# A new order for the DMA queue and the engine plan of a gated two-branch spectral mixer

## The chip, the cores and the metric

The kernel runs on one core of a Trainium2 chip. The metric is the device time of one execution in microseconds, as the median of several executions. A profile is one further execution; its span runs from the first to the last instruction and is about 2 us shorter than the device time. Runs that took over 1.5% longer than the fastest of the same kernel count as slow and are left out of all ratios. The engines are called TensorE (PE in the profile; its weight loads are PEld), VectorE (DVE), ScalarE (ACT), GpSimd (POOL) and SyncE (SP), which issues nearly all DMA. The hardware page set that readers have at hand is named "the Trainium skill", with the page's title.

## The reference, cut to what matters

```python
def _A_ref(x, w_r, w_i):                      # the same for B, with its own weights
    X = jnp.fft.rfft2(x.astype(jnp.float32), axes=(-2, -1))     # x: 1 x 2048 x 1024
    X = X * (w_r + 1j * w_i)
    return jnp.fft.irfft2(X, s=(2048, 1024), axes=(-2, -1)).astype(jnp.bfloat16)

g = sigmoid((x * gate_w).sum(-1, keepdims=True))
return g * A_ref(x) + (1 - g) * B_ref(x)
```

Both branches transform the same x, so the forward transform is done once and the two inverse ones are mixed by the gate before the last step.

## The kernel before

Every transform is a set of matmuls with constant matrices. The kernel has five steps, each in sixteen pieces:

- **f1**: first forward transform, straight from x. Its result needs sums and differences of column halves, done on VectorE ("fold"), on GpSimd ("pool") or by further matmuls ("sum").
- **f2, f3**: the rest of the forward transform, for the even half of the columns (units 0 to 7) and the odd half (units 8 to 15).
- **c1, c2, ce**: products with the spectral weights W on VectorE, and small corrections on GpSimd.
- **i1**: first inverse step. Its result is copied to SBUF and stored to a DRAM scratch (`hb`), from which it is read back in another layout (`rb`): half 0 into `re`, half 1 into `ro`.
- **i2, then ev, of, od, ol**: the gate and second inverse step on what was read back, then the last step and the stores (`st`).

The program is written out by hand. A plan lists the pieces, and each engine executes its instructions in the plan's order:

```python
PLAN = """
lw 3; lw 4; lw 5; f1 0; f1 3; ...            # lw: load weights W of a unit
... i1 7 1; f2 10 0; c1 8 w; hb 6; lw 15; ...
... i1> 13 1 A; i2 0 1; hb 12; c2 14 w; f3 15 w; f3> 15 w A; i2 0 0     # first readback units
"""
```

The pieces that the argument touches (cuts marked):

```python
def load_w(n):
    par, u = n // NU, n % NU
    k = n % 11                                # eleven slots: a later unit takes an earlier unit's slot
    ...
    nc.sync.dma_start(w, w_in[par][u].rearrange("p t a m -> p (t a) m"))

def i1_out(n):                                # hb: store of unit n to the scratch
    nc.sync.dma_start(HB[par][16 * u:16 * u + 16]. ... , PS.pop(("rl", n))[:])

def read_back(par, s0, n=2):                  # rb: slots s0 and s0 + 1 of half par
    nc.sync.dma_start(RR[par][:, s0:s0 + n, :], HB[par][:, s0:s0 + n, :])

def i2(par, v, eng="A"):                      # unit v reads slots 2v and 2v + 1
    for s in range(2):
        ps = one()[:]
        s1 = 2 * v + s
        for ch in range(4):
            for ab, Ew in enumerate((EA, EB)):
                nc.tensor.matmul(ps[:, ch * 128:ch * 128 + 128],
                                 lhsT=RR[par][:, s1, ...], rhs=Ew[:, s1, :], ...)     # line 543
        copy(eng[s % len(eng)], ...)

def pair(o, a, b, engs="DD"):                 # line 554: D = VectorE, P = GpSimd
    for k, op in enumerate((ALU.add, ALU.subtract)):
        (nc.vector if engs[k] == "D" else nc.gpsimd).tensor_tensor(o[:, :, k], a, b, op)
```

Of the kernel before, what the change touches and what calls it, by code (L numbers as in the profile page):

```python
# [12 lines left out]
D = 1024  # L13
# [122 lines left out]


F1_GROUPS = """
0 fold 0 0 2 0
1 pool 0 1 1 1  # L140
3 pool 1 1 1 s
2 fold 2 0 2 1
4 pool 2 1 1 s
6 fold 4 0 2 1
5 pool 3 1 1 s
7 fold 6 0 2 0
# [2 lines left out]
13 pool 5 1 1 s  # L149
10 fold 10 0 2 1  # L150
11 fold 12 0 2 0
14 sum 14 0 1 s
15 sum 15 0 1 s
16 pool 6 1 1 s
17 pool 7 1 1 s
18 fold 8 1 2 1
19 sum 10 1 2 1
20 sum 12 1 1 s
21 fold 13 1 1 0
22 fold 14 1 1 s  # L160
# [12 lines left out]
ce 2; f3 3 w; i1> 1 0 A; i1> 1 2 D; f2> 4 1 A; fs> 3; f3> 3 w A; i1> 1 1 A; f1+ 20; f1 23; c2 2 w; c1 3 w; f2 4 0
f1> 23 A; i1 2 0; ce 3; f2> 4 0 A; lw 6; hb 0; lw 8; f1+ 23; i1 2 1; c2 3 w; i1> 2 0 A; i1> 2 1 A; f3 4 w; lw 7; fs 4
lw 10; f3> 4 w A; f2 5 0; fs> 4; f2> 5 0 A; f2 5 1; i1> 2 2 D; f2> 5 1 A; c1 4 w; i1 3 0; hb 1; i1 3 1; i1> 3 0 A
ce 4; fs 5; f3 5 w; i1> 3 1 A; f3> 5 w A; hb 2; i1> 3 2 D; f2 6 0; fs> 5; f2> 6 0 A; f2 6 1; hb 3; i1 4 0; c2 4 w
lw 11; i1 4 1; f2> 6 1 D; f3 6 w; lw 12; i1> 4 0 A; c1 5 w; fs 6; f2 7 0; ce 5; i1> 4 2 D; fs> 6; f2 7 1; c2 5 w
i1 5 0; i1> 4 1 A; f3> 6 w A; lw 14; c1 6 w; hb 4; ce 6; ie; f2> 7 0 A; i1 5 1; f2> 7 1 A; fs 7; gh; i1> 5 0 A
i1> 5 2 D; fs> 7; i1> 5 1 A; f3 7 w; gh> A; f2 8 0; f3> 7 w A; f2 8 1; i1 6 0; hb 5; c2 6 w; i1 6 1; f2> 8 0 A
f2> 8 1 A; c1 7 w; i1> 6 0 A; i1> 6 1 A; lw 13; i1> 6 2 D; f3 8 w; f2 9 0; c2 7 w; f2 9 1; ce 7; f3> 8 w A; f2> 9 0 A  # L180
f2> 9 1 D; i1 7 0; i1 7 1; f2 10 0; c1 8 w; hb 6; lw 15; i1> 7 0 A; i1> 7 1 A; f3 9 w; i1 8 0; i1> 7 2 D; f3> 9 w A
f2 10 1; c2 8 w; i1 8 1; f2> 10 0 A; f2> 10 1 A; f2 11 1; f3 10 w; c1 9 w; i1> 8 0 A; i1> 8 2 D; f2 11 0; hb 7; rb 0 8
c2 9 w; i1> 8 1 A; i1 9 0; rb 0 0; i1 9 1; hb 8; f3> 10 w A; f2> 11 0 D; rb 0 4; f2> 11 1 A; i1> 9 0 A; rb 0 12
i1> 9 1 A; c1 10 w; i1> 9 2 D; f2 12 1; rb 0 10; hb 9; f2> 12 1 A; f3 11 w; f3> 11 w A; f2 12 0; f2> 12 0 A; i1 10 0
c2 10 w; rb 0 6; i1 10 1; f2 13 0; c1 11 w; i1> 10 0 A; i1> 10 2 D; f2 13 1; i1> 10 1 A; f3 12 w; i1 11 0; rb 0 2
f2> 13 0 A; f3> 12 w A; f2 14 0; c2 11 w; f2> 13 1 D; i1 11 1; gz 0 0; f2 14 1; i1> 11 0 A; hb 10; f3 13 w; c1 12 w
gz> 0; i1> 11 1 A; i1> 11 2 D; c2 12 w; f2> 14 1 D; gw 0; i1 12 0; f2> 14 0 D; rb 0 14; hb 11; f3> 13 w A; c1 13 w
c2 13 w; i1 12 1; i1> 12 0 A; i1> 12 1 A; f2 15 1; i1> 12 2 A; gw 1; f2 15 0; f2> 15 1 A; f3 14 w; f3> 14 w A
f2> 15 0 A; i1 13 0; i1 13 1; i1> 13 0 A; c1 14 w; i1> 13 1 A; i2 0 1; hb 12; c2 14 w; f3 15 w; f3> 15 w A; i2 0 0
i1> 13 2 D; i1 14 0; i1 14 1; i1> 14 0 A; gz 1 0; i1> 14 1 A; hb 13; c1 15 w; i1> 14 2 D; i2 0 2; i1 15 0; c2 15 w  # L190
i1 15 1; i1> 15 0 A; gz> 1; i1> 15 1 D; i1> 15 2 D; gw 2; phase; hb 14; i2 0 3; hb 15; ev 0 1; rb 1 0; rb 1 2; ev 1 0
i2 0 4; gw 3; ev 3 1; rb 1 8; i2 0 5; rb 1 4; ev 2 0; ev 4 1; i2 0 7; i2 0 6; i2 1 0; of 0 0; rb 1 12; i2 1 1; ev 5 1
rb 1 6; i2 1 2; of 1 1; i2 1 3; rb 1 10; st 0; rb 1 14; ev 6 0; of 2 1; ev 7 1; i2 1 4; od 3 0; i2 1 5; st 3; st 2
od 4 1; od 5 1; st 1; i2 1 6; st 4; st 5; i2 1 7; ol 6; ol 7
"""


# [484 lines left out]
```

## Time and profile before

| | before |
|---|---|
| device time, median of 3 runs | 126.56 us (125.37 to 126.69) |
| span of the profile | 123.9 us |
| first inverse product (i1) starts on TensorE | 26.05 us |
| first i2 unit of half 0 starts | 75.67 us |
| first i2 unit of half 1 starts | 94.84 us |
| busy: TensorE, VectorE, ScalarE, GpSimd | 86, 77, 71, 34% |

The chain, the waits and the queue of this kernel are shown and read in the prediction below.

### The profile page before, as it was taken

What the parts mean: (1) busy time and instruction counts of PE and PEld (TensorE: products, weight loads), DVE (VectorE), ACT (ScalarE), POOL (GpSimd) and SP (SyncE); (2) the same over time, 40 slices, a digit from 0 to 9 for tenths busy, and PEclk for the clock granted to TensorE, in tenths of its full rate; (3) what the DMA queues carried; (4) which work ended last, traced back from release to release, by engine and by line L of the source; (5) the groups of instructions that cost most, each with busy time, mean ns of one, the idle gap of its engine ahead of it and who ended that gap; (6) DMA issues with size and microseconds to landing.
All of it is one profiled execution on the core that took longest, in us unless ns stands there. A gap on an engine that the chain in (4) does not pass through costs nothing.

```text
span 123.9 us, 3786 instructions
## 1 busy us (share of the span) xinstructions
PE 106.5 (86%) x1582; PEld 71.8 (58%) x1582; DVE 95.5 (77%) x139; ACT 88.5 (71%) x140; POOL 41.9 (34%) x58
## 2 busy tenths in 40 slices
PE   6999999998889899999896835999997999999700
PEld 2799996863545434534354405767986898656200
DVE  0089987799998995999999994275895368999820
ACT  4068466587989998999998992779968696606300
POOL 1059957361135555200000000000000099996520
PEclk9999999999999999999999995599999999999996
DMA  3999999999997899997499999905479921841994
GB/s 94 310 393 415 376 405 409 392 404 398 405 400 253 231 284 368 401 400 285 83 312 418 398 402 393 356 23 177 167 257 415 413 108 50 295 171 50 403 385 177
DMA packets 18289, 37.41 MB, mean 302 GB/s; under 512 B 1756, under 2 KB 10848, under 8 KB 18272
## 3 DMA queue, kind: packets, MB, share of 16 engines
q1 hardware_dynamic: 17808, 36.97, 80.8%
q10 hardware_dynamic: 432, 0.20, 0.6%
q8 instruction: 12, 0.20, 0.6%
q14 instruction: 5, 0.04, 0.1%
q0 software_dynamic: 32, 0.01, 0.0%
HBM read 24.58 MB, written 12.58 MB: 300 GB/s over the span
## 4 chain that ended last, share of the span: by engine, by line
PE 50%; DVE 15%; DMA 12%; ACT 11%; issue 5%; SPq 1%; DVEq 1%; ACTq 0%
PE ps L543 10%; DMA re<-h_143 9%; PE ia L514 5%; PE ps L425 3%; ACT rl L307 3%; PE ps L303 3%; ACT y L307 3%; DMA re<-in_x_dram 3%; DVE re L554 3%; DVE rl L307 2%; PE ps L334 2%; PE ib L514 2%; DVE T L307 2%; ACT X_149 L307 2%; ACT X_150 L307 2%
## 5 line engine op out<-in xcount | busy, mean ns | idle before, releaser
L554 POOL TENSOR_TENSOR ot<-re,y 128x1024 bf16<-128x1024 f32 x6 | 14.0, 2373 | 49.2 <-DVE y L554 49.2
L307 ACT CAST y<-ps 128x512 bf16<-128x512 f32 x35 | 19.3, 597 | 9.3 <-PE ps L543 7.7
L307 ACT CAST rl<-ia 128x1024 bf16<-128x1024 f32 x16 | 16.2, 1013 | 2.7 <-PE ib L514 2.3
L425 PE MATMUL ps<-fd,y 128*128 128x256 bf16 x112 | 16.3, 273 | 1.8 <-DVE T L307 0.8
L425 PEld LDWEIGHTS <-y 128*128 128x128 bf16 x128 | 11.0, 97 | 8.4 <-issue 7.0
L303 PEld LDWEIGHTS <-re 128*128 128x128 bf16 x216 | 13.1, 102 | 1.9 <-DMA re<-in_x_dram 1.2
L514 PEld LDWEIGHTS <-wi 32*64 32x64 bf16 x512 | 6.9, 104 | 9.5 <-issue 5.8
L543 PE MATMUL ps<-ea,re 128*128 128x128 bf16 x64 | 9.6, 242 | 3.2 <-DMA re<-h_143 2.8
L307 DVE CAST rl<-ib 128x512 bf16<-128x512 f32 x16 | 10.9, 686 | 1.8 <-PE ib L514 1.7
L307 ACT CAST T<-ps 128x512 bf16<-128x512 f32 x20 | 11.8, 613 | 0.6 <-PE ps L425 0.6
L543 PEld LDWEIGHTS <-re 128*128 128x128 bf16 x128 | 9.0, 110 | 4.7 <-DMA re<-h_143 3.3
L543 PE MATMUL ps<-eb,re 128*128 128x128 bf16 x64 | 9.7, 243 | 0.0
L564 PEld LDWEIGHTS <-y 128*128 128x128 bf16 x88 | 8.2, 97 | 2.0 <-issue 0.6
L307 ACT CAST rl<-ib 128x512 bf16<-128x512 f32 x16 | 9.4, 595 | 0.0
L462 PEld LDWEIGHTS <-wf 64*64 64x64 bf16 x192 | 4.9, 108 | 7.2 <-issue 5.4
L543 PEld LDWEIGHTS <-ro 128*128 128x128 bf16 x128 | 7.8, 98 | 1.3 <-issue 0.7
L543 PE MATMUL ps<-ea,ro 128*128 128x128 bf16 x64 | 8.1, 219 | 0.4 <-ACT y L307 0.4
L543 PE MATMUL ps<-eb,ro 128*128 128x128 bf16 x64 | 8.1, 219 | 0.0
L303 PE MATMUL ps<-f_89,re 128*128 128x128 bf16 x72 | 5.6, 222 | 0.4 <-DVE e_781 L451 0.4
L307 DVE CAST T<-ps 128x512 bf16<-128x512 f32 x8 | 5.5, 687 | 0.2 <-PE ps L425 0.2
L334 PEld LDWEIGHTS <-re 128*128 128x128 bf16 x80 | 4.6, 98 | 0.0
L291 DVE TENSOR_SCALAR gh<-gws 128x8 f32<-128x8 bf16 x1 | 0.2, 172 | 5.3 <-DMA gws<-in_gw_dram 5.3
(298 smaller groups left out, 262.9 us busy)
## 6 DMA issues: line engine op xcount, KB each, us to landing
h_143<-rl SPq DMA_DIRECT2D x8, 512.0 KB, 5.9
re<-h_143 SPq DMA_DIRECT2D x8, 512.0 KB, 9.2
h_144<-rl SPq DMA_DIRECT2D x8, 512.0 KB, 8.2
ro<-h_144 SPq DMA_DIRECT2D x8, 512.0 KB, 5.7
re<-in_x_dram SPq DMA_DIRECT2D x6, 512.0 KB, 7.2
out_dram<-ot SPq DMA_DIRECT2D x6, 512.0 KB, 3.6
ro<-in_we_dram SPq DMA_DIRECT2D x5, 512.0 KB, 8.2
ro<-in_wo_dram SPq DMA_DIRECT2D x5, 512.0 KB, 7.4
```

The costliest lines, as they stand in the source:

```text
L291: nc.vector.tensor_scalar(gh[:], gws[:], 0.25, None, ALU.mult)
L303: nc.tensor.matmul(o[:, q * 128:(q + 1) * 128], lhsT=x[:, s1, h * 512 + q * 128:h * 512 + (q + 1) * 128], rhs=F1[:, h * e, :], start=(h == ...
L307: (nc.scalar.copy if eng == "A" else nc.vector.tensor_copy)(out=out, in_=in_)
L334: nc.tensor.matmul(o, lhsT=x[:, s1 + s, h * 512 + (q + 2 * a) * 128:h * 512 + (q + 2 * a) * 128 + 128], rhs=F1[:, (h * e + a * r) % 2, :], ...
L425: nc.tensor.matmul(ps[:, i * 512 + q // 2 * 256:i * 512 + q // 2 * 256 + 256], lhsT=y[:, par, q, 4 * u + 2 * t:4 * u + 2 * t + 2, :, :].re ...
L462: nc.tensor.matmul(ps[hp(jh ^ tt), i * 512 + dst:i * 512 + dst + ln], lhsT=WF[hp(jh), 2 * u + tt, w, :], rhs=T[hp(jh), tt, src:src + ln], ...
L514: nc.tensor.matmul(bank[g][hp(tt)], lhsT=WI[h, 2 * u + tt, w, :], rhs=p[h, 4 * tt + row:4 * tt + row + 2, o:o + 256], start=(r == k == 0), ...
L543: nc.tensor.matmul(ps[:, ch * 128:ch * 128 + 128], lhsT=RR[par][:, s1, c0 + 256 * ab:c0 + 256 * ab + 128], rhs=Ew[:, s1, :], start=(ab == ...
L554: (nc.vector if engs[k] == "D" else nc.gpsimd).tensor_tensor(o[:, :, k], a, b, op)
L564: nc.tensor.matmul(ps[:, o:o + 256], lhsT=V[:, s, 2 * r + a, :], rhs=rhs[:, 2 * r + a, 0:256], start=(a == 0), stop=(a == 1))
```

## The change

The stated intent: each W load is issued right behind the product that frees its slot, each unit's scratch store right behind its copies, and the scratch is read back in the order of use. The diff rewrites the whole plan, and shifts some work between engines on the way. Its core, with the plan reduced to the words concerned and cuts marked:

```diff
 F1_GROUPS                       # group, kind, slot, half, count, accumulator
-23 fold 15 1 1 s
+23 sum 15 1 1 s
 ...                             # other accumulators for groups 0, 4, 14, 17
 PLAN, DMA queue only, in order
-lw 3 4 5; fd; lw 9 6; hb 0; lw 8 7 10; hb 1; hb 2; hb 3; lw 11 12 14; hb 4; ie; hb 5; lw 13; hb 6; lw 15; hb 7
-rb 0 8; rb 0 0; hb 8; rb 0 4; rb 0 12; rb 0 10; hb 9; rb 0 6; rb 0 2; hb 10; rb 0 14; hb 11; hb 12; ...
+lw 3 4 5 6; fd; lw 10 7 8; hb 0; lw 11 9; hb 1; lw 12 13 14; hb 2; hb 3; lw 15; ie; hb 4; hb 5; hb 6; hb 7
+rb 0 2; rb 0 0; rb 0 4; hb 8; hb 9; rb 0 6; rb 0 8; hb 10; rb 0 10; rb 0 14; hb 11; hb 12; rb 0 12; ...
 PLAN, GpSimd's folds of the opening, in order
-f1+ 1; f1+ 3; f1+ 5; f1+ 4; f1+ 13; f1+ 12; f1+ 16; ws; f1+ 17
+f1+ 4; f1+ 1; f1+ 3; f1+ 13; ws; f1+ 16; f1+ 5; f1+ 12; f1+ 17
 PLAN, the end
-of 0 0; ... of 1 1; ... of 2 1; ... od 3 0; ... od 4 1; od 5 1; ...
+of 0 1 PD; ... of 1 1 PP; ... of 2 1; ... od 3 0; ... od 4 1; of 5 0 DP; ...
```

The order of the i2 units of half 0 is about the same in both: 1, 0, 2, 3, 4, 5, 7, 6.

More of the change, by code (lines that the diff above doesn't have):

```diff
@@ L138 @@
 F1_GROUPS = """
-0 fold 0 0 2 0
+0 fold 0 0 2 1
 1 pool 0 1 1 1
@@ L142 @@
 2 fold 2 0 2 1
-4 pool 2 1 1 s
+4 pool 2 1 1 0
 6 fold 4 0 2 1
@@ L151 @@
 11 fold 12 0 2 0
-14 sum 14 0 1 s
+14 sum 14 0 1 1
 15 sum 15 0 1 s
 16 pool 6 1 1 s
-17 pool 7 1 1 s
+17 pool 7 1 1 0
 18 fold 8 1 2 1
@@ L160 @@
 22 fold 14 1 1 s
-23 fold 15 1 1 s
+23 sum 15 1 1 s
 """
 PLAN = """
-lw 3; lw 4; lw 5; f1 0; f1 3; f1 1; f1 4; f1> 0 A; f1+ 0; f1> 1 A; f1 2; f1> 2 D; f1> 4 A; f1 6; f1+ 1; f1> 3 A
-f1> 6 A; f1 5; f1+ 2; f1+ 3; f1> 5 A; f1 7; f1+ 5; f1+ 6; f1+ 4; f1> 7 A; f1 12; f1+ 7; f1 8; f1> 12 A; f1 13; f1> 8 A
-f1 10; f1 11; f1> 13 A; f1+ 8; f1> 10 A; f1+ 10; f1+ 13; f1> 11 D; f1 14; f1+ 12; f1 15; f1> 14 A; f1> 15 A; f1 16
-f1 18; f1+ 11; f1> 18 D; f1+ 18; f1 17; f1> 16 A; f1+ 15; f1> 17 A; f2 0 0; f2 1 w; f1+ 16; ws; f1+ 17; f2 0 1
@@ L169 @@
-f2> 0 1 D; f2> 0 0 A; f3 0 0; f3> 0 0 A; f1+ 14; f3 0 1; fs 0; f3> 0 1 D; f2> 1 w A; f1 19; c1 0 0; f1> 19 A; fs 1
-f3 1 w; fs> 1; c1 0 1; fs> 0; f2 2 w; f3> 1 w A; c2 0 w; ce 0; f1 20; c1 1 w; f2> 2 w A; f1 21; f1> 21 A; phase
-f1> 20 A; i1 0 0; ce 1; i1 0 1; fs 2; fd; f1 22; i1> 0 0 A; f1+ 19; f1+ 21; i1> 0 1 A; i1> 0 2 D; fs> 2; f3 2 w
-c2 1 w; f2 3 1; f3> 2 w A; f1> 22 A; f2> 3 1 D; f1+ 22; lw 9; c1 2 w; i1 1 0; f2 3 0; f2> 3 0 A; i1 1 1; f2 4 1; fs 3
-ce 2; f3 3 w; i1> 1 0 A; i1> 1 2 D; f2> 4 1 A; fs> 3; f3> 3 w A; i1> 1 1 A; f1+ 20; f1 23; c2 2 w; c1 3 w; f2 4 0
@@ L174 @@
-f1> 23 A; i1 2 0; ce 3; f2> 4 0 A; lw 6; hb 0; lw 8; f1+ 23; i1 2 1; c2 3 w; i1> 2 0 A; i1> 2 1 A; f3 4 w; lw 7; fs 4
-lw 10; f3> 4 w A; f2 5 0; fs> 4; f2> 5 0 A; f2 5 1; i1> 2 2 D; f2> 5 1 A; c1 4 w; i1 3 0; hb 1; i1 3 1; i1> 3 0 A
-ce 4; fs 5; f3 5 w; i1> 3 1 A; f3> 5 w A; hb 2; i1> 3 2 D; f2 6 0; fs> 5; f2> 6 0 A; f2 6 1; hb 3; i1 4 0; c2 4 w
-lw 11; i1 4 1; f2> 6 1 D; f3 6 w; lw 12; i1> 4 0 A; c1 5 w; fs 6; f2 7 0; ce 5; i1> 4 2 D; fs> 6; f2 7 1; c2 5 w
-i1 5 0; i1> 4 1 A; f3> 6 w A; lw 14; c1 6 w; hb 4; ce 6; ie; f2> 7 0 A; i1 5 1; f2> 7 1 A; fs 7; gh; i1> 5 0 A
@@ L179 @@
-i1> 5 2 D; fs> 7; i1> 5 1 A; f3 7 w; gh> A; f2 8 0; f3> 7 w A; f2 8 1; i1 6 0; hb 5; c2 6 w; i1 6 1; f2> 8 0 A
-f2> 8 1 A; c1 7 w; i1> 6 0 A; i1> 6 1 A; lw 13; i1> 6 2 D; f3 8 w; f2 9 0; c2 7 w; f2 9 1; ce 7; f3> 8 w A; f2> 9 0 A
-f2> 9 1 D; i1 7 0; i1 7 1; f2 10 0; c1 8 w; hb 6; lw 15; i1> 7 0 A; i1> 7 1 A; f3 9 w; i1 8 0; i1> 7 2 D; f3> 9 w A
-f2 10 1; c2 8 w; i1 8 1; f2> 10 0 A; f2> 10 1 A; f2 11 1; f3 10 w; c1 9 w; i1> 8 0 A; i1> 8 2 D; f2 11 0; hb 7; rb 0 8
-c2 9 w; i1> 8 1 A; i1 9 0; rb 0 0; i1 9 1; hb 8; f3> 10 w A; f2> 11 0 D; rb 0 4; f2> 11 1 A; i1> 9 0 A; rb 0 12
@@ L184 @@
-i1> 9 1 A; c1 10 w; i1> 9 2 D; f2 12 1; rb 0 10; hb 9; f2> 12 1 A; f3 11 w; f3> 11 w A; f2 12 0; f2> 12 0 A; i1 10 0
-c2 10 w; rb 0 6; i1 10 1; f2 13 0; c1 11 w; i1> 10 0 A; i1> 10 2 D; f2 13 1; i1> 10 1 A; f3 12 w; i1 11 0; rb 0 2
-f2> 13 0 A; f3> 12 w A; f2 14 0; c2 11 w; f2> 13 1 D; i1 11 1; gz 0 0; f2 14 1; i1> 11 0 A; hb 10; f3 13 w; c1 12 w
-gz> 0; i1> 11 1 A; i1> 11 2 D; c2 12 w; f2> 14 1 D; gw 0; i1 12 0; f2> 14 0 D; rb 0 14; hb 11; f3> 13 w A; c1 13 w
-c2 13 w; i1 12 1; i1> 12 0 A; i1> 12 1 A; f2 15 1; i1> 12 2 A; gw 1; f2 15 0; f2> 15 1 A; f3 14 w; f3> 14 w A
@@ L189 @@
-f2> 15 0 A; i1 13 0; i1 13 1; i1> 13 0 A; c1 14 w; i1> 13 1 A; i2 0 1; hb 12; c2 14 w; f3 15 w; f3> 15 w A; i2 0 0
-i1> 13 2 D; i1 14 0; i1 14 1; i1> 14 0 A; gz 1 0; i1> 14 1 A; hb 13; c1 15 w; i1> 14 2 D; i2 0 2; i1 15 0; c2 15 w
-i1 15 1; i1> 15 0 A; gz> 1; i1> 15 1 D; i1> 15 2 D; gw 2; phase; hb 14; i2 0 3; hb 15; ev 0 1; rb 1 0; rb 1 2; ev 1 0
-i2 0 4; gw 3; ev 3 1; rb 1 8; i2 0 5; rb 1 4; ev 2 0; ev 4 1; i2 0 7; i2 0 6; i2 1 0; of 0 0; rb 1 12; i2 1 1; ev 5 1
-rb 1 6; i2 1 2; of 1 1; i2 1 3; rb 1 10; st 0; rb 1 14; ev 6 0; of 2 1; ev 7 1; i2 1 4; od 3 0; i2 1 5; st 3; st 2
@@ L194 @@
-od 4 1; od 5 1; st 1; i2 1 6; st 4; st 5; i2 1 7; ol 6; ol 7
+lw 3; lw 4; lw 5; f1 0; f1 1; f1 3; f1> 0 A; f1+ 0; f1> 1 A; f1 4; f1> 4 A; f1 2; f1> 3 A; f1 6; f1> 2 D; f1 5
+f1> 6 A; f1+ 2; f1> 5 A; f1 12; f1 7; f1+ 6; f1 8; f1 13; f1> 7 A; f1+ 4; f1> 12 A; f1+ 7; f1 10; f1> 8 A; f1 11
+f1+ 1; f1+ 8; f1> 13 A; f1 14; f1 15; f1+ 3; f1> 10 A; f1> 11 D; f1+ 10; f1+ 13; ws; f1> 14 A; f1> 15 A; f1+ 11; f1 18
+f1+ 15; f1 16; f1> 16 A; f1> 18 D; f1 17; f2 0 0; f1+ 18; f2 0 1; f1> 17 A; f1+ 14; f2> 0 0 A; f1+ 16; f2 1 w
@@ new lines @@
+f2> 0 1 A; f3 0 0; f3 0 1; f3> 0 0 A; f1+ 5; f1 19; f3> 0 1 D; c1 0 0; f2> 1 w A; fs 1; lw 6; fd; c1 0 1; fs 0; fs> 1
+f1> 19 A; f1+ 12; f3 1 w; fs> 0; f2 2 w; f3> 1 w A; f2> 2 w A; c2 0 w; lw 10; f1 20; f1+ 17; phase; c1 1 w; ce 0
+f1 21; f1> 20 A; i1 0 0; i1 0 1; fs 2; f1+ 19; f1> 21 A; lw 7; lw 8; i1> 0 0 A; f1+ 21; i1> 0 2 D; i1> 0 1 A; hb 0
+f3 2 w; f3> 2 w A; ce 1; fs> 2; f2 3 1; f1 22; c2 1 w; lw 11; f1> 22 A; f2> 3 1 D; f1+ 22; i1 1 0; f2 3 0; f2> 3 0 A
+i1 1 1; f2 4 1; fs 3; f3 3 w; c1 2 w; fs> 3; ce 2; f1 23; lw 9; i1> 1 0 A; f1+ 20; f2> 4 1 A; i1> 1 1 A; f2 4 0
@@ new lines @@
+f3> 3 w A; f1> 23 A; i1> 1 2 D; hb 1; c2 2 w; lw 12; lw 13; c1 3 w; i1 2 0; ce 3; f2> 4 0 A; i1 2 1; f1+ 23; f3 4 w
+i1> 2 0 A; fs 4; c2 3 w; lw 14; f2 5 0; f3> 4 w A; fs> 4; i1> 2 1 A; f2> 5 0 A; i1> 2 2 D; hb 2; f2 5 1; f2> 5 1 A
+i1 3 0; c1 4 w; i1 3 1; i1> 3 0 A; fs 5; ce 4; i1> 3 2 D; f2 6 1; f3 5 w; i1> 3 1 A; hb 3; f3> 5 w A; f2 6 0; i1 4 0
+f2> 6 0 A; fs> 5; c2 4 w; lw 15; i1 4 1; f2> 6 1 D; c1 5 w; f3 6 w; i1> 4 0 A; fs 6; f2 7 1; i1> 4 2 D; fs> 6; c2 5 w
+ie; ce 5; f2 7 0; i1> 4 1 A; hb 4; i1 5 0; f3> 6 w A; i1 5 1; gh; f2> 7 0 A; c1 6 w; f2> 7 1 D; fs 7; i1> 5 0 A; ce 6
@@ new lines @@
+i1> 5 2 D; i1> 5 1 A; hb 5; f3 7 w; f2 8 1; gh> A; fs> 7; f3> 7 w A; f2 8 0; i1 6 0; c2 6 w; i1 6 1; f2> 8 1 A
+f2> 8 0 A; i1> 6 0 A; i1> 6 1 A; c1 7 w; ce 7; f2 9 0; f3 8 w; i1> 6 2 D; hb 6; c2 7 w; f2 9 1; i1 7 0; f3> 8 w A
+i1 7 1; f2> 9 1 D; f2 10 0; f2> 9 0 A; c1 8 w; i1> 7 0 A; f3 9 w; i1 8 0; i1> 7 2 D; i1> 7 1 A; hb 7; f2 10 1; c2 8 w
+f3> 9 w A; c1 9 w; f2> 10 0 A; i1 8 1; f2> 10 1 A; f2 11 1; f3 10 w; i1> 8 0 A; i1> 8 2 D; f2 11 0; c2 9 w; rb 0 2
+rb 0 0; i1 9 0; rb 0 4; i1> 8 1 A; hb 8; i1 9 1; f2 12 1; f3> 10 w A; f2> 11 0 D; f2> 11 1 A; i1> 9 0 A; c1 10 w
@@ new lines @@
+i1> 9 2 D; i1> 9 1 A; hb 9; f3 11 w; rb 0 6; f3> 11 w A; f2 12 0; f2> 12 1 A; c2 10 w; i1 10 0; rb 0 8; i1 10 1
+f2> 12 0 A; c1 11 w; i1> 10 0 A; i1> 10 2 D; f2 13 0; i1> 10 1 A; hb 10; f2 13 1; f2> 13 0 A; f3 12 w; i1 11 0
+f3> 12 w A; rb 0 10; c2 11 w; i1 11 1; f2> 13 1 D; i1> 11 0 A; gz 0 0; rb 0 14; f2 14 1; c1 12 w; f2 14 0; i1 12 0
+i1> 11 2 D; i1> 11 1 A; hb 11; c2 12 w; f3 13 w; gz> 0; f2> 14 1 D; f3> 13 w A; f2> 14 0 D; c1 13 w; c2 13 w; i1 12 1
+f2 15 1; i1> 12 0 A; i1> 12 2 A; f2 15 0; i1> 12 1 A; hb 12; f2> 15 1 A; rb 0 12; f3 14 w; i1 13 0; gw 0; f3> 14 w A
@@ new lines @@
+f2> 15 0 A; i1 13 1; c1 14 w; i1> 13 0 A; gw 1; i2 0 1 A; i1> 13 1 A; c2 14 w; i1> 13 2 D; hb 13; f3 15 w; f3> 15 w A
+c1 15 w; i2 0 0; i1 14 0; i1 14 1; i1> 14 0 A; i1> 14 2 D; gz 1 0; i1> 14 1 A; hb 14; i2 0 2 A; i1 15 0; c2 15 w
+i1 15 1; i1> 15 0 A; gz> 1; i1> 15 1 D; i1> 15 2 D; hb 15; gw 2; i2 0 3 DA; phase; ev 0 1; rb 1 0; ev 1 0; i2 0 4
+gw 3; ev 3 1; rb 1 2; rb 1 4; i2 0 5 A; ev 4 1; i2 0 7; ev 2 0; rb 1 6; i2 0 6; i2 1 0 A; of 0 1 PD; i2 1 1; rb 1 8
+ev 5 1; rb 1 10; rb 1 12; i2 1 2; of 1 1 PP; i2 1 3 DA; ev 6 0; ev 7 1; of 2 1; i2 1 4; rb 1 14; od 3 0; i2 1 5; st 0
@@ L195 @@
+od 4 1; of 5 0 DP; st 3; st 2; st 1; i2 1 6 A; st 4; i2 1 7; st 5; ol 6; ol 7
 """
```

## The prediction

> **What bounds the kernel now.** I read the page's slices first, then busy time by stretch, the chain that ended last, the waits and the DMA queue's order. No engine bounds the whole span of 123.9 us. From 20 to 72 us VectorE and ScalarE are nearly full (18.6 and 19.3 of the 20 us from 40 to 60) and TensorE follows them; from about 85 to 113 us TensorE is nearly full; at the end it is the output stores. Between the second and third of these lies a hole.
>
> ```profile
> PEclk9999999999999999999999995599999999999996
> ```
>
> Each digit is one fortieth of the span, 3.1 us, and shows the granted TensorE clock in tenths. Two slices from 74 us run at about half. The busy table of the same place (columns PE, PEld, DVE, ACT, POOL, clock, DMA share, GB/s):
>
> ```profile
> 65.00:70.00 5.00, 3.51 (x77) 2.00 (x62) 4.97 (x9) 4.35 (x6) 0.00 (x0) 1.00 1.04 407
> 70.00:75.00 5.00, 2.37 (x48) 0.92 (x47) 4.97 (x6) 4.42 (x8) 0.00 (x0) 0.92 1.06 406
> 75.00:80.00 5.00, 4.33 (x43) 3.51 (x44) 1.14 (x3) 2.52 (x4) 0.00 (x0) 0.50 1.07 386
> 80.00:85.00 5.00, 5.00 (x105) 3.08 (x102) 3.29 (x4) 3.80 (x7) 0.00 (x0) 0.90 0.27 93
> ```
>
> VectorE is full until 75 us, then nearly empty: 1.14 of 5. ScalarE halves. TensorE looks busy from 75 to 80 us only because the clock is 0.50. DMA is at its ceiling (about 406 GB/s) until 80 us, then idles. The chain that ended last says why (start, duration, what):
>
> ```profile
> 64.32 11.30 DMA re<-h_143
> 75.62 0.05 issue
> 75.67 1.89 PE ps L543 x16
> 77.56 1.00 PE pt_1759 L462 x9
> ```
>
> h_143 is the DRAM scratch of half 0; the second transform (line 543, called i2 in the plan) reads it back transposed. Its first unit waited for a readback that was 11.3 us in flight. Two waits result, the second being the knock-on (X_150 comes out of the product that stands behind i2 on TensorE):
>
> ```profile
> PE ps L543 <- DMA re<-h_143: 2.8, 1, 2.8
> DVE p_1842 L483 <- ACT X_150 L307: 3.9, 1, 3.9
> ```
>
> The queue's own order shows the reason for the late readback:
>
> ```profile
> 59.57 0.80 SPq L374 DMA_DIRECT2D re<-h_143  x2
> 60.47 0.37 SPq L529 DMA_DIRECT2D h_144<-rl  x1
> 60.88 2.06 SPq L374 DMA_DIRECT2D re<-h_143  x3
> 63.05 0.42 SPq L529 DMA_DIRECT2D h_144<-rl  x1
> 63.51 1.23 SPq L374 DMA_DIRECT2D re<-h_143  x2
> ```
>
> The plan reads back slots 8, 0, 4, 12, 10, 6, 2, 14, but the first i2 unit needs slot 2, the seventh. Six other readbacks and two stores, 8 x 524 KB = 4.2 MB, stand before it, and with its own 0.5 MB that is 11.6 us at 406 GB/s from about 61 us: hence 75.6.
>
> **What the Trainium skill says.** "TensorE: Matmul & The Clock Gate", Part 1: The HAM clock gate, says that TensorE falls to half clock after an idle window of about 3.4 us and needs a busy one to recover. Here the weight-load side was idle 3.3 us, the matmuls 2.8 us, and the clock was 0.50 for some 6 us. It agrees, and it means that the stall is paid twice. "DMA: Bandwidth & Descriptors", Queues, rings and completion order, says that an engine's descriptors of one queue are consumed in ring order; this agrees with the seventh readback landing after what stood ahead. The same page, Two DMAs through the same engine are not ordered, asks for a completion wait before a transfer reads what another wrote: so no readback can start before the last of the eight stores has landed. The trace agrees: store 7 is issued at 53.87, the first readback at 59.57, with 5.2 us of waiting put down to the store.
>
> **The change, part by part.** It is a new order of the same work with some reassignments.
>
> 1. Readback order becomes 2, 0, 4, 6, 8, 10, 14, 12, and i2 uses units 1, 0, 2, 3, 4, 5, 7, 6: the order of use. Slot 2 is now first: issued at about 58 to 59.5 us it lands by 65, far before TensorE reaches i2 at 72.9. That removes the 2.8 us stall and the half clock. What this is worth is read from the path behind it. Rescheduling from 72 us by durations: product 14 first factor and gate weights on VectorE to 74.1, second factor to 75.2, one copy to 75.8. ScalarE in its new order: copy of unit 13 (0.9 pitch), two y copies, one 0.5 copy, X_150 done about 76.5. So product 15 starts at 76.5 instead of 79.70, its second factor ends near 79.5 instead of 83.67, the last inverse matmuls near 80.1 instead of 84.45, the gate sigmoid near 81.9 instead of 86.36. That is 4.4 us: 2.8 of stall and about 1.6 of slow matmuls. TensorE itself lost 2.3 us to half clock (two i2 units at 1.89 and 1.82 against 0.89, one product at 1.00 against 0.6), but not all of it comes back, as ScalarE is next to fill up: 7.6 us of copies from 73.2 to 81.
>
> 2. Stores right behind their copies, W loads right behind the product that frees the slot. In the queue before, three stores in a row (33.97 to 40.3 us) held the W loads behind them, and DMA fell to some 230 to 285 GB/s there. But no product waits for a W transfer anywhere in the list of waits, so the earlier W is worth 0 by itself. Its use is an emptier queue when store 7 goes out: perhaps 5.7 us to landing becomes 4, readbacks start 1.5 us earlier, which part 1 has already hidden. Worth 0, as insurance.
>
> 3. Opening: one fold group becomes a sum on TensorE (eight more matmuls of about 56 ns, 0.45 us, where TensorE has room), which takes two VectorE adds (0.66 us of pitch) away and gives ScalarE 0.2 us. One T copy goes to ScalarE (0.48), another comes back. VectorE is the fuller engine in most of 20 to 72 us, so I count 0.7 us; I expect the new order of folds to be neutral, as the folds that feed the first unit still end near 17 us.
>
> 4. End. Units 0 and 5 of the last step: unit 5 is folded, 0.87 us of matmuls instead of 1.73; GpSimd's subtraction of unit 0 goes to VectorE; two y copies go from ScalarE to VectorE. VectorE gains about 1.2 + 0.6 + 0.6 = 2.4 us of work, of which one 0.6 copy is outside the crowded stretch. GpSimd is what times the stores before:
>
> ```profile
> 99.44 13.98 POOL L554 TENSOR_TENSOR ot<-re,y 128x1024 bf16<-128x1024 f32 x6 [49.16 <-DVE y L554]
> 109.31 7.00 SPq L618 DMA_DIRECT2D out_dram<-ot  x5
> ```
>
> Six operations of 2.33 us run to 113.4; the store of unit 2 waits for the last and three more stand behind it, so 3.1 MB leave after 113.4, 7.8 us at 400 GB/s, ending at 123.9 with landing. After: five such operations before the store of unit 2, started 4.4 us earlier, but with unit 2's inputs ready near 102.5: about 107.6. VectorE, summed by its new order from 93.5 us (fold pairs 1.2, full pairs 2.3, copies 0.6), ends at 113.5 to 114 against 118.65, TensorE at 111.2 against 116.1. So this stage keeps the 4.4 us and adds 0.5 to 1.2.
>
> Sum: 4.4 + 0.7 + 0.8 = 5.9 us; less about 0.4 for small waits that a new order always opens: 5.5 us. The span should be near 118.4 and the time 126.56 - 5.5 = 121.0.
>
> **Rivals.** (a) The stall goes but the time hardly falls, because DMA is the bound from 60 to 80 us: eight readbacks and eight stores are 8.4 MB, 21 us at 400 GB/s, and half 1's readback needs all eight stores landed. For it: share 1.04 to 1.07 for 15 us. Against it: DMA idled from 80 to 85 us, store 15 took only about 3.5 us, and first use of half 1 came 5.4 us after its first readback was issued. If it held, half the gain would go: about 124. (b) The end gives it back: VectorE, with 1.8 us more in the last 20 us, becomes the bound, or the stores still leave in one burst. Then 4 us remain of it: 122.5. (c) A queue in program order: an early store or W load waits for its product and holds a readback behind it. Slots 6 and 8 stand behind the store of unit 9 and slots 10 and 14 behind that of unit 10, but those issued at 63 and 65.4 us before, and slot 6 is first used after 80. I give it little; a second stall of 2 us would make it 123.5. (d) The middle stage gets slower by the new order, by 1 to 2 us: 122 to 123. (e) Everything helps, readbacks and stores both ahead: 119.
>
> **Range and chances.** The removal of the stall is nearly certain, its worth of 3.5 to 4.5 us fairly so; the rest is plus or minus 1.5 us. The 2% line is 124.03, which takes a gain of 2.5 us. Only (a), or (c) with (d), miss it. So 121.0, 8 in 10 between 119.0 and 123.8; faster 0.87, same 0.10, slower 0.03.
>
> **What would show it.** Right: no wait of L543 on h_143, granted clock full between 70 and 85 us, VectorE idle before the last products below 1.5 us instead of 3.9, half 1's first readback issued near 85 instead of 89.4, GpSimd's first ot near 95, store of unit 2 near 108. Wrong: a clock of 0.5 that has moved elsewhere, L543 waiting for h_144, VectorE still working at 118 us, or stores ending more than 5 us after the last VectorE instruction.

## The result, and the profile after

The changed kernel took 121.95 us as the median of 4 runs (121.77 to 122.58), beside 126.16 us (125.37 to 126.69) for the kernel before. The ratio is 0.968, with a 95% interval of 0.961 to 0.975. All ratios in this document are the mean time of one kernel's fast runs over that of the other's of the same rounds, so they are not quite the ratio of the medians quoted beside them. Ratios of different chips are not compared to less than a per cent.

The clock row of the page of the changed kernel, the answer to the one with two half-speed slices:

```profile
PEclk9999999999999999999999999999999999999985
```

The half clock in the middle is gone. The busy table of the same four stretches (PE, PEld, DVE, ACT, POOL, clock, DMA share, GB/s):

```profile
65.00:70.00 5.00, 4.81 (x97) 2.42 (x96) 4.79 (x6) 4.19 (x7) 0.00 (x0) 1.00 1.07 399
70.00:75.00 5.00, 4.70 (x81) 2.25 (x66) 4.77 (x7) 5.00 (x8) 0.00 (x0) 1.00 1.04 400
75.00:80.00 5.00, 4.29 (x84) 2.97 (x82) 4.93 (x8) 4.83 (x8) 0.00 (x0) 1.00 0.93 337
80.00:85.00 5.00, 4.90 (x81) 3.67 (x79) 3.53 (x6) 4.63 (x9) 0.00 (x0) 1.00 0.62 208
```

VectorE works through to 80 us (4.93 of 5, where it had 1.14), and ScalarE is now the fullest engine from 70 to 80 us (9.83 of 10, VectorE 9.70). The DMA queue of the changed kernel (start, duration of the issue, what):

```profile
58.70 1.55 SPq L374 DMA_DIRECT2D re<-h_143  x3
60.36 2.03 SPq L529 DMA_DIRECT2D h_144<-rl  x2
62.44 2.21 SPq L374 DMA_DIRECT2D re<-h_143  x2
...
86.70 3.84 SPq L374 DMA_DIRECT2D ro<-h_144  x8
```

Slots 2, 0 and 4 are the first three, issued from 58.70 us; the first i2 unit runs at 73.95 us and waits for no transfer. Half 1's first readback is issued at 86.70 us instead of 89.39. But something else is new. The waits of TensorE in the changed kernel (engine, line, what it waited for: us in total, times, longest) begin with

```profile
PE ia L514 <- POOL p_534 L496: 2.0, 1, 2.0
```

and the opening of GpSimd shows where that comes from. First the kernel before, then the changed one (start, duration, what; at_ is the copy that a fold reads, e_ and p_ are the small corrections):

```profile
14.59 1.43 POOL L312 TENSOR_TENSOR y<-at_316 128x256 bf16<-128x256 f32 x2
17.33 1.42 POOL L312 TENSOR_TENSOR y<-at_454 128x256 bf16<-128x256 f32 x2 [1.31 <-ACT at_454 L307]
...
19.60 1.41 POOL L312 TENSOR_TENSOR y<-at_456 128x256 bf16<-128x256 f32 x2
```

```profile
19.14 1.41 POOL L312 TENSOR_TENSOR y<-at_441 128x256 bf16<-128x256 f32 x2 [2.12 <-ACT at_441 L307]
...
23.71 2.84 POOL L312 TENSOR_TENSOR y<-at_467 128x256 bf16<-128x256 f32 x2
26.52 1.20 POOL L493 TENSOR_TENSOR e_607<-X_149,wh 128x16 f32<-128x16 bf16 x1
27.79 0.23 POOL L496 TENSOR_TENSOR p_534<-e_607,e_565 128x8 bf16<-128x8 f32 x1
```

Before, the last fold was over at 21.0 us. In the changed kernel GpSimd first waits 2.12 us for the copy of group 16, whose matmuls now stand behind those of group 18, and three more folds (5, 12, 17) stand behind it; the last ends at 26.5 us. Only then does the correction come that the first inverse product needs. The last fold (two operations) also takes 2.84 us instead of 1.41: it runs beside VectorE's first products, and these are slow too. In VectorE's timeline two products of 128x1024 take 2.39 us together in the changed kernel, where one took 0.68 us before (the kernel before first):

```profile
21.73 0.68 DVE L483 TENSOR_TENSOR p_542<-X_149,w_116 128x1024 bf16<-128x1024 bf16 x1
```

```profile
21.91 2.39 DVE L483 TENSOR_TENSOR p_534<-X_149,w_116 128x1024 bf16<-128x1024 bf16 x2
```

At the end of the changed kernel GpSimd's timeline is this:

```profile
96.17 3.27 POOL L554 TENSOR_TENSOR ot<-re,y 128x1024 bf16<-128x1024 f32 x1 [44.09 <-DVE y L554]
99.83 9.33 POOL L554 TENSOR_TENSOR ot<-re,y 128x1024 bf16<-128x1024 f32 x4 [0.39 <-DVE y L554]
109.97 3.35 POOL L554 TENSOR_TENSOR ot<-re,y 128x1024 bf16<-128x1024 f32 x1 [0.81 <-ACT y L307]
113.28 2.48 POOL L607 TENSOR_TENSOR ot<-re,y 128x512 bf16<-128x512 f32 x2
```

The first five operations (units 0, 1, 2) end at 109.2 instead of 113.4 us. Two of the six take 3.3 us where each took 2.37 before; each of the two has VectorE's own operation of the same unit beside it. GpSimd is now the compute engine that ends last, at 115.8 us; VectorE ends at 114.7 (before: 118.7), and the stores end at 120.0.

### The profile page after: what moved, and what is told of

It is laid out like the page before. It is cut to its first block, busy times and chain, and to the rows that moved or that the text cites. A ratio compares the mean times of both kernels' runs of the same rounds, so it can differ in the third digit from the quotient of the medians.

```text
span 120.0 us, 3811 instructions
## 1 busy us (share of the span) xinstructions
PE 104.9 (87%) x1588; PEld 71.2 (59%) x1590; DVE 98.9 (82%) x141; ACT 87.6 (73%) x139; POOL 45.3 (38%) x58
## 4 chain that ended last, share of the span: by engine, by line
PE 38%; DMA 17%; POOL 11%; ACT 9%; DVE 9%; issue 8%; POOLq 1%; SPq 1%; ACTq 0%; DVEq 0%
DMA re<-in_x_dram 8%; PE ps L543 7%; DMA w_116<-in_wo_dram 6%; POOL y L312 5%; PE ia L514 4%; POOL ot L554 4%; PE ps L425 3%; PE ib L514 3%; DVE rl L307 3%; ACT rl L307 3%; ACT X_149 L307 3%; DMA f_89<-cst_f 2%; PE ps L386 2%; POOLq L677 1%; PE pt_2315 L588 1%
## 5 line engine op out<-in xcount | busy, mean ns | idle before, releaser
L554 POOL TENSOR_TENSOR ot<-re,y 128x1024 bf16<-128x1024 f32 x6 | 15.9, 2681 | 45.3 <-DVE y L554 44.5
L307 ACT CAST y<-ps 128x512 bf16<-128x512 f32 x33 | 18.4, 610 | 2.0 <-PE ps L543 1.7
L425 PEld LDWEIGHTS <-y 128*128 128x128 bf16 x128 | 10.9, 97 | 7.5 <-issue 6.2
L564 PEld LDWEIGHTS <-y 128*128 128x128 bf16 x96 | 8.9, 98 | 2.1 <-issue 0.6
L543 PE MATMUL ps<-ea,re 128*128 128x128 bf16 x64 | 8.4, 219 | 0.3 <-ACT y L307 0.2
L543 PE MATMUL ps<-eb,re 128*128 128x128 bf16 x64 | 8.3, 219 | 0.0
L312 POOL TENSOR_TENSOR y<-at_204 128x256 bf16<-128x256 f32 x2 | 1.4, 728 | 7.6 <-ACT at_204 L307 7.6
L238 PE MATMUL ps<-warm 128*128 128x512 bf16 x6 | 2.7, 630 | 1.2 <-DVE warm L235 1.2
```

The source lines that it names most:

```text
L238: nc.tensor.matmul(wps[:], lhsT=warm[:, 0:128], rhs=warm[:], start=True, stop=True)
L307: (nc.scalar.copy if eng == "A" else nc.vector.tensor_copy)(out=out, in_=in_)
L312: eng.tensor_tensor(o, av, bv, op)
L425: nc.tensor.matmul(ps[:, i * 512 + q // 2 * 256:i * 512 + q // 2 * 256 + 256], lhsT=y[:, par, q, 4 * u + 2 * t:4 * u + 2 * t + 2, :, :].re ...
L543: nc.tensor.matmul(ps[:, ch * 128:ch * 128 + 128], lhsT=RR[par][:, s1, c0 + 256 * ab:c0 + 256 * ab + 128], rhs=Ew[:, s1, :], start=(ab == ...
L564: nc.tensor.matmul(ps[:, o:o + 256], lhsT=V[:, s, 2 * r + a, :], rhs=rhs[:, 2 * r + a, 0:256], start=(a == 0), stop=(a == 1))
```

## The experiments

The theory after the first reading: the readback order alone gives the whole gain, by two costs removed (the wait and the half clock); the new places of stores and W loads give little; the new engine order loses about 2 us in the opening, by GpSimd's folds, and wins some of it back later. The main rivals: the gain comes from the earlier stores and W loads, or from the new engine order.

All milestones are from the profiles, in us. Each row shows one profiled execution. Columns: first inverse product; first i2 unit of half 0; first i2 unit of half 1; end of the span; then the median time of the fast runs and the ratio to the kernel before of the same rounds.

| kernel | i1 | i2, half 0 | i2, half 1 | end | time | ratio |
|---|---|---|---|---|---|---|
| before | 26.05 | 75.67 | 94.84 | 123.9 | 126.16 | |
| changed | 28.07 | 73.95 | 91.58 | 120.0 | 121.95 | 0.968 |
| b_rb | 26.60 | 73.33 | 91.00 | 120.1 | 122.01 | 0.972 |
| b_hblw | 25.89 | 75.33 | 93.62 | 122.7 | 123.46 | 0.986 |
| b_allsp | 26.55 | 73.28 | 91.33 | 120.4 | 121.75 | 0.968 |
| b_warm | 26.16 | 75.50 | 92.40 | 121.5 | 123.96 | 0.988 |
| a_oldrb | 28.86 | 78.75 | 96.25 | 124.6 | 125.92 | 1.002 |
| a_pool | 26.03 | 72.01 | 89.65 | 118.0 | 120.00 | 0.955 |
| a_of0 | 27.83 | 74.75 | 92.41 | 121.5 | 123.14 | 0.981 |
| a_again | 27.95 | 74.84 | 92.49 | 120.9 | 122.19 | 0.976 |
| a_pool_2 | 26.14 | 72.14 | 89.78 | 118.2 | 120.01 | 0.958 |
| a_pool_od5 | 27.20 | 73.19 | 90.83 | 118.9 | 119.21 | 0.951 |
| a_pool_od5_2 | 26.09 | 72.08 | 89.73 | 117.8 | 119.48 | 0.954 |
| a_pool_od5_of0 | 26.59 | 72.58 | 90.22 | 119.5 | 120.93 | 0.964 |

All of them gave the right result. The names that begin with b_ are edits of the kernel before, those with a_ of the changed one.

### b_rb: the readback order alone

```diff
 PLAN of the kernel before, same places
-rb 0 8; rb 0 0; rb 0 4; rb 0 12; rb 0 10; rb 0 6; rb 0 2; rb 0 14
+rb 0 2; rb 0 0; rb 0 4; rb 0 6; rb 0 8; rb 0 10; rb 0 14; rb 0 12
```

> The kernel before with nothing changed but which slots the eight readbacks of half 0 fetch: 2, 0, 4, 6, 8, 10, 14, 12 in place of 8, 0, 4, 12, 10, 6, 2, 14. My theory: the readback order alone carries the gain; L543 no longer waits for h_143, the granted clock stays at 1.00 from 70 to 80 us, and the time falls by 3.5 to 4.5 us, to 121.7 to 122.7. Rival A (the gain needs the early stores and W loads): under 1.5 us, above 124.7. Rival B (the new engine order with its sums, folds and hand-overs carries it): also under 1.5 us.

Measured: 122.01 us beside 125.08 for the kernel before, ratio 0.972 (0.966 to 0.978). That is 3.5 us by the ratio and 3.1 by the medians, the lower edge of what was expected. Its busy table:

```profile
70.00:75.00 5.00, 4.03 (x77) 2.21 (x76) 4.97 (x7) 5.00 (x9) 0.00 (x0) 1.00 1.05 402
75.00:80.00 5.00, 4.51 (x96) 3.03 (x103) 4.33 (x5) 5.00 (x9) 0.00 (x0) 1.00 1.07 388
```

The clock is 1.00 and VectorE and ScalarE are busy through the former hole. From the first inverse product to the first i2 unit of half 1 the kernel before took 94.84 - 26.05 = 68.79 us, this one 91.00 - 26.60 = 64.40: 4.4 us less, for six changed numbers (slots 0 and 4 keep their places). Both rivals fall for the larger part. That the profile shows more than the times has a likely reason: the profiled execution of the kernel before has a mean clock of 0.965, while five of the seven runs of that kernel beside b_rb have 0.973 to 0.978, so in these the half clock was probably shorter.

### b_hblw: stores and W loads alone

```diff
 PLAN of the kernel before: lw, hb, fd, ie in the order and places of the changed kernel;
 readbacks in the changed kernel's places, but with the old slots
+hb 7; rb 0 8; rb 0 0; rb 0 4; hb 8; hb 9; rb 0 12; rb 0 10; hb 10; rb 0 6; rb 0 2; hb 11; hb 12; rb 0 14
```

The edit also takes over the places of the output stores and the order in which half 1 is read back (2, 4, 6, 8 ... in place of 2, 8, 4, 12 ...). In its profile the stretch from half 1's first i2 unit to the end is as long as before (29.1 us), so these two show no effect here.

> The kernel before with the W loads and scratch stores in the changed kernel's queue order, but the old slots in the readbacks. My theory: nothing to gain, as no product waited for a W load: the stall of 2.8 us stays, give or take 1 us from readbacks issued earlier, and the time is 125.2 to 126.5. Rival A: 122 to 124.

Measured: 123.46 us, fast runs from 122.87 to 124.63, ratio 0.986 (0.976 to 0.995): 1.8 us by the ratio. The median is 1.7 us below the range; the expectation missed. The first readback was issued at 56.6 instead of 59.6 us, but the wait stayed at 2.65 us, as slot 2 is still the seventh readback and now stands behind one more store. What was shorter is the half clock: 0.66 in the mean from 75 to 80 us instead of 0.50. In this trace the first i2 unit still began at full speed; the granted clock was 0.50 from about 75.8 to 79.2 us (3.4 us), against 74.2 to 81.0 us (6.8 us) before. The mean clock of each run points the same way: the fast run at 0.976 took 124.63 us, and the kernel before took 124.81 to 126.30 us at 0.973 to 0.978; the two fast runs at 0.986 took 122.87 and 123.46 us. So most of the 1.8 us seems to lie in a shorter half clock. Why the clock fell less in these runs, and whether the earlier stores are the reason, stays open.

### b_allsp: the whole new queue order on the old engine order

```diff
 PLAN of the kernel before: all DMA words in the order of the changed kernel, at their earliest places
```

> The kernel before with the changed kernel's whole queue order (W loads, stores, readbacks) and the old order on the compute engines. My theory: as b_rb alone within 0.7 us, 121.5 to 122.7, so equal to the changed kernel, the new engine order being worth about nothing net. Rival B: clearly slower than the changed kernel, above 124.

Measured: 121.75 us, ratio 0.968 (0.960 to 0.976), beside 0.972 for b_rb on the same chip: the same within the intervals. With the readbacks in order of use, earlier stores and W loads add at most a few tenths, which these runs do not resolve. It also equals the changed kernel's 0.968, so within the per cent to which chips can be compared the engine order of the changed kernel is worth nothing net.

### a_oldrb: the changed kernel with the old slots

```diff
 PLAN of the changed kernel, same places
-rb 0 2; rb 0 0; rb 0 4; rb 0 6; rb 0 8; rb 0 10; rb 0 14; rb 0 12
+rb 0 8; rb 0 0; rb 0 4; rb 0 12; rb 0 10; rb 0 6; rb 0 2; rb 0 14
```

> The changed kernel with the readbacks of half 0 fetching the old slots 8, 0, 4, 12, 10, 6, 2, 14 in the new places of the queue. My theory (readback order carries the gain): L543 waits for h_143 again, and longer than before, as the seventh readback now stands behind more stores: 2 to 5 us of wait with a half clock after it; time 124.5 to 128, against 121.95. Rival (the new engine order has slack at this point): under 123.

Measured: 125.92 us, ratio 1.002 (0.991 to 1.012). The whole gain is gone. The wait is back in its list of waits:

```profile
PE ps L543 <- DMA re<-h: 2.9, 1, 2.9
```

So the order of these eight readbacks carries the gain in both kernels, under both plans.

### b_warm: the wait without the half clock

```diff
-i1> 13 1 A; i2 0 1
+i1> 13 1 A; wm; i2 0 1
+    def keep_warm():
+        ps = one()
+        for _ in range(12):
+            nc.tensor.matmul(ps[:], lhsT=F1[:, 0, :], rhs=FD[:, 0, 0:2, :].rearrange("p a b -> p (a b)"), start=True, stop=True)
```

> The kernel before with twelve spare 128x512 matmuls (0.22 us each, 2.6 us, result unused) on TensorE just ahead of its first readback unit, so that it is busy while it waits. My theory: the readback still lands at 75 to 76 us, but the granted clock stays at or near 1.00 from 75 to 80, i2 units take 0.9 us not 1.85, and the time falls by 1.2 to 2 us, to 123.5 to 124.8. Rival (only the wait costs, the slow matmuls lie beside ScalarE's work): within 0.5 us of the kernel before.

Measured: 123.96 us beside 125.20, ratio 0.988 (0.981 to 0.994): 1.6 us by the ratio, 0.7 to 2.4 by its interval, so clear of no change although under 2%. Its busy table:

```profile
70.00:75.00 5.00, 4.39 (x57) 1.96 (x58) 4.97 (x7) 4.53 (x8) 0.00 (x0) 1.00 1.06 406
75.00:80.00 5.00, 5.00 (x97) 3.51 (x95) 2.68 (x4) 3.84 (x6) 0.00 (x0) 1.00 1.07 384
```

The spare matmuls ran from 72.9 to 75.5 us, and the first i2 unit began right behind them at 75.50, as late as before. The readbacks were issued as before (the first at 59.47 us, before 59.57); TensorE waited for none, so when the data landed doesn't show. But the clock stayed at 1.00, and VectorE got 2.68 us of work from 75 to 80 us instead of 1.14. The half clock alone therefore cost 1.6 us by the ratio; between the first i2 units of the two halves it is 94.84 - 75.67 = 19.2 us before and 92.40 - 75.50 = 16.9 here, 2.3 us in the profiled execution.

### a_pool: GpSimd's folds of the opening back in the gap

```diff
 PLAN of the changed kernel
-ws; f1> 14 A; ... f1+ 16; ... f1+ 5; ... f1+ 12; ... f1+ 17
+ws; f1+ 5; f1+ 12; f1> 14 A; ... f1+ 16; ... f1+ 17
```

> The changed kernel with two GpSimd folds of the opening (groups 5 and 12) put back ahead of the fold of group 16, into the 2.1 us in which GpSimd waits at 17 to 19 us. My theory: the changed kernel lost 2 us in the opening, as the folds ran late and beside VectorE's products, both slowed; now the first inverse product starts near 26 us, not 28.1, products take 1.2 us, and the time falls by 1 to 2 us to 120 to 121. Rival: the 2 us were this run's slower loads (store of x landed later), or are absorbed by slack later: within 0.4 us of 121.95.

Measured: 120.00 us, ratio 0.955. In its GpSimd timeline the four folds (two operations each) run through without the wait and at their usual pace (folds started 1.38 us apart in the kernel before, so four take 5.5 us):

```profile
16.84 5.54 POOL L312 TENSOR_TENSOR y<-at 128x256 bf16<-128x256 f32 x8
```

The first inverse product starts at 26.03 us instead of 28.07, and the 2.0 us stay to the end: 72.01 against 73.95, 89.65 against 91.58, 118.0 against 120.0. As chips differ, it was run again beside the changed kernel:

> The changed kernel once more, as the reference on this chip for the three beside it. Expected: 0.965 to 0.975 of the kernel before; the wait of the first inverse product for GpSimd's p, near 2 us, there again.

> a_pool once more on the same chip as the changed kernel. My theory: 1.2 to 2.2 us less than the changed kernel, and no wait of the first inverse product for GpSimd. Rival (the 2 us between two jobs were the chip): within 0.5 us.

Measured on one chip: 122.19 us (0.976, just outside the expected 0.965 to 0.975) for the changed kernel and 120.01 us (0.958) for a_pool, 2.2 us less. The rival that the lost 2 us were one run's slow loads falls. a_again shows one thing more. This is the clock row of its page:

```profile
PEclk9999999996899999999999999999999999999985
```

Its wait of 1.9 us at 26 to 28 us was followed by a clock of 0.50 from 28.0 to 31.4 us, and it reached the first i2 unit 0.9 us later than in the first profile of the changed kernel, which had the same wait and a full clock.

### a_of0, a_pool_od5, a_pool_od5_2, a_pool_od5_of0: the end

```diff
 a_of0: the changed kernel with
-of 0 1 PD
+of 0 1 PP
 a_pool_od5 (twice): a_pool with
-of 5 0 DP
+od 5 0
 a_pool_od5_of0: both
```

> The changed kernel with both final operations of unit 0 on GpSimd, as before. My theory (a VectorE operation with both inputs in SBUF blocks GpSimd): the first GpSimd operation takes 2.33 us, not 3.27; unit 5's, which still has such a neighbour, stays at 3.3. Time within 0.7 us of the changed kernel, as GpSimd gets one operation more (2.33) and loses 0.94. Rival (the first operation is slow for another reason, a cold start): it stays at 3.27.

> The changed kernel with the opening's folds moved as in a_pool, and unit 5 of the end not folded (full matmuls, both sums on VectorE), as in the kernel before. My theory: GpSimd ended last in a_pool (113.8 us, stores to 118.0), by way of unit 5's 3.35 us operation; without it its last two come 0.4 to 1.1 us earlier, for 0.87 us more of TensorE: 119.0 to 120.0 against a_pool's 120.0. Rival (TensorE sets the end): slower than a_pool by 0.3 to 0.9 us.

> a_pool with unit 5 not folded, once more on one chip with a_pool. In the last job GpSimd then waited before its last two operations, so VectorE sets the end. Expected 0 to 0.8 us less than a_pool_2.

> The same with unit 0's subtraction back on GpSimd as well. My theory: no VectorE operation with two SBUF inputs remains beside GpSimd's, so all six of GpSimd's take 2.33 us; VectorE has 1.15 us less to do and ends about 0.5 to 1 us earlier, GpSimd's six end near 109.5; time 0.2 to 0.8 us under a_pool_od5_2. Rival (the store of unit 2, then later by 0.8 us, sets the end): equal or up to 0.5 us slower.

GpSimd's operations on ot, from the list of one tile (durations in ns as shortest/median/longest), in a_of0 and then in a_pool_od5_of0:

```profile
L554 POOL TENSOR_TENSOR ot<-re,y x7: 2368/2386/3390, 97.0 to 110.9; 128x1024 bf16<-128x1024 f32 x7
```

```profile
L554 POOL TENSOR_TENSOR ot<-re,y x6: 2340/2356/2368, 94.8 to 106.4; 128x1024 bf16<-128x1024 f32 x6
```

With unit 0's neighbour gone only unit 5's operation is slow; with both gone none is. So the slow ones are slow because of VectorE's operation beside them, which reads two operands from SBUF. The skill says this too: "SBUF — State Buffer", Who interferes with whom, has a VectorE instruction with two SBUF inputs contend with a GpSimd instruction that reads SBUF. The trace agrees, at +0.9 to 1.0 us per GpSimd operation.

For the time this contention is the smaller matter, and here my expectation failed. a_of0 took 123.14 us, ratio 0.981 (0.974 to 0.987; the changed kernel's 0.976 on another chip lies within); from the first i2 unit of half 1 to the end it needed 121.5 - 92.41 = 29.1 us, against 120.9 - 92.49 = 28.4 in a_again. a_pool_od5_of0 took 120.93 us, 1.45 more than a_pool_od5_2 beside it, and 29.3 us for the same stretch against 117.8 - 89.73 = 28.1; even the rival in its expectation had allowed 0.5 us at most. All of GpSimd's operations ran at full pace and VectorE had less to do, and still it was slower. The traces put the reason in the queue's stores; no run moved these alone (first a_pool_od5_2, then a_pool_od5_of0):

```profile
97.62 12.61 SPq L618 DMA_DIRECT2D out_dram<-ot  x6
```

```profile
99.53 12.15 SPq L618 DMA_DIRECT2D out_dram<-ot  x6
```

With two operations of unit 0 in a row on GpSimd, unit 0's store goes out 1.9 us later, and the store of unit 2, for which units 1, 4 and 5 wait in the queue, becomes possible 1.5 us later, as GpSimd's last 128x1024 operation ends at 108.8 instead of 107.3 (0.5 us of each is the later start of this execution). VectorE ends 4.2 us before the end of the span in one and 5.5 us in the other. VectorE gained nothing from the lighter load: it now waits twice 0.48 us for ScalarE's copies of TensorE's results and ends 23.8 us after half 1's first i2 unit in both. Handing half of unit 0 to VectorE is a good move although it slows GpSimd's other half.

a_pool_od5 took 119.21 us (0.951) in its first job and 119.48 us (0.954) beside a_pool's 120.01 (0.958) in the second: 0.5 us less, as expected. Unit 5's 3.35 us operation no longer stands before GpSimd's last two, which start at 110.93 instead of 111.47 us and now wait for VectorE. It is the fastest version found: 119.48 against 122.19 us for the changed kernel and 125.60 for the kernel before, all on one chip.

## Why the prediction was right or wrong

The forecast was 121.0 us, 119.0 to 123.8; measured were 121.95. The direction and most of the mechanism held; one step failed, and it makes up most of the difference.

**Readback order (4.4 us): right.** b_rb alone shortened the stretch from the first inverse product to half 1's first i2 unit by 4.4 us in the profile, and a_oldrb took all of it away again. By the ratio of times it was 3.5 us. The split into 2.8 for the wait and 1.6 for the slow matmuls fits less well. b_warm, which keeps the clock and starts i2 as late as before, saved 1.6 us by the ratio; in the profile it shortened the same stretch to 92.40 - 26.16 = 66.24 us, which is 2.5 of the 4.4 us. Either way about 1.9 us are left for the wait. Milestones such as half 1's first readback came 1.7 us later than forecast (86.7 instead of 85), because the whole trace was late from the opening on (84.53 in a_pool).

Two readings behind this part don't come out. The queue's 11.6 us from 61 us end at 72.6, not at 75.6: at 406 GB/s the queue moved some 5.9 MB from 61 to 75.6 us, 1.2 MB more than the nine transfers counted. Two more had been issued by 66.8 us and others followed from 69.47 us; whether theirs were the extra bytes these runs don't show. And the clock fell at 74.2 us, only 1.3 us after TensorE's last matmul had ended (72.9), so TensorE had not been idle for the 3.4 us with which the prediction found the trace in agreement.

**Stores and W loads (0): right in the kernel as changed.** Beside the right readback order they add nothing that was resolved (b_allsp against b_rb). With the old slots b_hblw was 1.8 us below its kernel before by the ratio, with a shorter half clock; that part is not settled.

**Opening and middle (+0.7): this step failed.** It said: "I expect the new order of folds to be neutral, as the folds that feed the first unit still end near 17 us". I had looked at VectorE's folds, which feed the forward transform. The first inverse product also needs a small GpSimd correction, and GpSimd is in order: the folds of other groups stand before it. Moving group 16's matmuls behind group 18's made GpSimd idle for 2.1 us, moving two folds behind group 16's made them run late, and then they ran beside VectorE's products with two SBUF operands, which slowed both (2.84 instead of 1.41 us for a fold's two operations, 2.39 instead of 1.36 for two products). TensorE waited 2.0 us. a_pool, which moves two words of the plan, gave back 2.0 to 2.2 us. The middle did gain: from the first inverse product to half 1's first i2 unit the changed kernel took 91.58 - 28.07 = 63.51 us, 0.9 us less than b_rb's 64.40 (63.6 in all five a_pool profiles; 64.5 in a_again and a_of0, where the clock fell in the opening). So the term of +0.7 was -2.0 + 0.9 = -1.1.

**End (0.5 to 1.2 us on top): right in size, partly for another reason.** From half 1's first i2 unit to the end it took 28.42 us instead of 29.06, 0.6 us less. I had VectorE as the last engine; it was GpSimd, by 1.1 us, as two of its operations took 3.3 us each. The skill's SBUF page would have told me; I did not look it up. One of the signs of being wrong came true by this: the stores ended 5.3 us after the last VectorE instruction (120.0 against 114.7), where I had set 5. a_of0 and a_pool_od5_of0 show that giving half of unit 0 to VectorE was worth 0.7 to 1.2 us all the same, by earlier stores, and a_pool_od5_2 that folding unit 5 cost 0.5 us in a_pool.

**The sum:** 4.4 - 1.1 + 0.6 = 3.9 us, the difference of the spans (123.9 - 120.0). It has to be, as the terms are differences of the same milestones. Of the rivals, (a) and (b) and (c) did not occur: the share of the DMA engines was still 1.04 to 1.07 from 65 to 75 us, but it held nothing up once the first transfers were the ones needed. Rival (d) had the right size in the wrong place: the new order made the opening slower, not the middle.

## What to carry to other kernels

When a buffer is written and read back in pieces, queue the pieces in the order of first use: a needed transfer that stands seventh in a full queue comes after what stands before it, and the wait can be paid a second time in TensorE's clock. When a plan is rewritten, follow the in-order queue of every engine up to each small operation that something big waits for, GpSimd's too. Before moving work between VectorE and GpSimd, ask which of them delays the first store, and look whether VectorE then reads two operands from SBUF while GpSimd reads SBUF too.

## What the Trainium skill lacked or had wrong

- "SBUF — State Buffer", Who interferes with whom, calls the shared ports an exclusive lock under which the second instruction fully blocks. At the end of the kernel a GpSimd operation that began 0.1 to 0.2 us into a VectorE operation of 1.23 us grew by 0.9 to 1.0 us, which fits. In the opening both engines were slow when they alternated: two VectorE products took 2.39 us instead of 1.36 and the two operations of a GpSimd fold 2.84 instead of 1.41. The page gives no duration for such a run of operations on both sides.
- "TensorE: Matmul & The Clock Gate", Why this matters for your kernels, advises against idle gaps above about 3 us. Here gaps of 2.65, 2.81 and 2.91 us (b_hblw, before, a_oldrb) led to the half clock, and a gap of 1.9 to 2.0 us did so in three profiles of the changed opening (a_again, a_of0, a_oldrb) but not in a fourth with the same gap. The half clock then lasted 6.8 us in the kernel before and 3.4 us in the five other cases.
- No page that I read treats a store queue in which one engine's late result holds back finished ones. Here a result of GpSimd that came 1.5 us later (1.0 net of the later start) went with an end that came 1.2 us later for the same stretch.
